# An attention, experts and feed-forward kernel on one core: six tiles for the factors made in the experts, a store on another queue, and other begin times for conversions

## The chip, the cores and the metric

The kernel runs on one core of a Trainium2 chip. The core has five engines that work side by side, each through an instruction queue of its own: TensorE (PE in the profile, its weight loads apart as PEld), VectorE (DVE), ScalarE (ACT), GpSimd (POOL) and SyncE (SP), which only issues transfers. An instruction waits at the head of its queue until the semaphores that it names have come, and what stands behind it on the same engine waits too. The metric is device time in microseconds, the median of several runs. The chip grants TensorE a clock at one of two levels, 1.2 or 2.4 GHz; the profile writes them as 0.50 and 1.00 of full speed.

## The reference, cut to what matters

```python
# q, k, v: (4, 8, 576, 64)
scores = 1.0 / np.sqrt(64) * np.matmul(q, k.transpose(0, 1, 3, 2))
thresh = np.max(scores, axis=-1, keepdims=True) - tau
scores = np.where(scores >= thresh, scores, -1000000000.0)
attn = softmax(scores)
x = np.matmul(attn, v) as (2304, 512)                  # tokens by model width

expert_idx = np.argmax(xn @ en.T / mtau, axis=1)       # one of 8 experts a token
for e in range(8):
    mask = expert_idx == e
    out[mask] = gate_w[mask, None] * (np.maximum(x[mask] @ w1[e], 0) @ w2[e])   # 512 -> 1024 -> 512

h = out @ w_in                                         # 512 -> 2048
g = np.maximum(h, 0.0) + alpha * np.minimum(h, 0.0)
return g @ w_out                                       # 2048 -> 512
```

w_in and w_out come as 64-bit floats; the kernel reads them as pairs of 32-bit words and turns them into float32 with integer operations ("conversion" below).

## The kernel before

**Products in two parts.** A float32 operand is kept as two tiles of a reduced type (fp32r): a high part, which ScalarE writes by a cast, and a low part, which GpSimd or VectorE writes as the difference of the value and its high part. A product takes three matmuls: high x high, high x low, low x high.

**Three stages.** Attention runs to about 354 us of the span, the experts from there to 641, the feed-forward network ("the network") to 1053; the rest is the end of the last stores.

**Experts.** There are 8 experts of fixed capacity (432, 256, 384, 256, 368, 272, 320 and 288 columns, in the order in which they run), each with 8 feature blocks: 64 groups g = 8 r + f. In group g, `l1(g)` multiplies by a block of w1, `relu` makes the high part `h` on ACT (L1209) and the low part on VectorE (L1210), and `l2(g-1)` multiplies the `h` of the group before by a block of w2 (L1257 to L1259). `wsplit` makes the high and low parts of the weights (L1124, L1138, L1139). After the last block the result is copied to `yT` (L1268, L1269) and `yout` (L1279) stores it in DRAM at a place that is read from `meta_i` first (L1278); both go through SP's queue. For the last expert that happens after the loop.

Preparations for the network are strewn between the groups. `conv` (conversion of w_in, L1605 to L1646) is called at fixed groups. Everything that stands in the list `early` has a due time in groups, given by `at(due, step)`, and is emitted in the loop as soon as g has reached it. In this list are the **factors**: the network multiplies by sums and differences of quarters of w_in, seven a pair of feature blocks, each 128 x 512 with both parts. For four of the eight pairs they are made here. `sums` forms them; `factor(i, p)` then has three steps: a cast of the high part on ACT (L1696), the subtraction on GpSimd (L1698), the store to the DRAM tensor `ws` by SP (L1700). Each takes a tile of `wtile`, here from a pool `wf` of two:

```python
for x, p in enumerate((1, 2, 4, 6, 7, 5, 3)):
    f = run(lambda i=i, p=p: factor(i, p))
    for y in range(3):
        at(g0 + 2.2 + 1.1 * x + 0.5 * y, f)
```

Later entries of `early` fetch the network's first inputs and call `weights` (L1711) five times, which loads a factor back from `ws` into the pool `wr` of `NR` = 6 tiles.

**Network.** It goes in six visits, `VISITS = ((0,0), (1,0), (2,0), (2,1), (1,1), (0,1))`: (block q of 768 tokens, half of the feature pairs), four pairs a visit. A pair takes seven products (`prod`, L1869, in the order p = 1, 2, 6, 7, 5, 3, 4, six matmuls of 384 columns each) which run up in two PSUM banks `ha` and `hb`; after each, the load of the factor that is needed five products later is issued (`weights`). ACT keeps partial results by copies `v`, `w`, `d` (L1878). `act` applies the activation with its alpha (`u` and `c`, L1891 to L1902), then ACT casts the high part `gh` (L1913) and GpSimd makes the low part `gl` (L1918). The output products (`f2mm`, L1985 to L1987, nine matmuls for one feature block and half a token block) of the pair or of the one before stand between the seven products. After the last feature block `evac` scales by the gate weight and `put` (L1950) or a plain store writes the rows.

Side work is held in chains of steps. `tick(us)` is called after each product (1.05) and after each set of output products (2.08 each feature block) and emits the next step or steps of each chain, as far as a small account of each engine's time allows; a step of kind "N" does nothing and ends the chain's turn for this tick. `finish(name)` emits at once whatever is left of a chain, where its result is needed. Two kinds of chains matter here. `wout(c)` converts one row block of w_out: a load (L2003), then nine steps on ACT, VectorE and GpSimd (L1605 to L1618), of which L1612 on ACT writes the high part and L1617 and L1618 on GpSimd the low part of `wo`. No more than two of them are open at a time. `factors(i)` makes the factors of one of the other four pairs: step k of nine casts factor k on ACT (L2041), subtracts for factor k - 1 on GpSimd (L2045) and stores factor k - 2 (L2047); its tiles come from a pool `wf` of three. The table `work` says in which visit, and at which pair, a chain is queued.

## Time and profile before

| | |
|---|---|
| timed runs, us | 1060.70, 1063.87, 1064.52 (median 1063.87) |
| the profiled execution: time / span, us | 1062.55 / 1060.6 |
| TensorE busy | 977.0 us, 92% of the span |
| VectorE busy | 785.4 us, 74% |
| ScalarE busy | 619.9 us, 58% |
| GpSimd busy | 682.7 us, 64% |
| mean granted clock of TensorE | 0.97 |

The span runs from the first instruction to the last of the one execution that the profiler recorded; the time of the same execution is 1.95 us longer. Busy times leave out waiting, so the shares say only which engine has least to spare over the whole. Where an engine stood still, and for whom, is read from the views by stretch, from the list of waits and from the timeline. There an idle time stands in brackets behind the instruction that ended it, with an arrow to what released it. Several matmuls of one line are drawn together as "x6"; ends of matmuls are modelled.

### The profile page before, as it was taken

To read this page: it belongs to the slowest core of one execution; us is meant where nothing else is said; L and a number is where in the kernel's file an instruction comes from. 1 tells how busy PE (TensorE), PEld (TensorE's weight loads), DVE (VectorE), ACT (ScalarE), POOL (GpSimd) and SP (SyncE) were. 2 spreads that over 40 slices of the span, in tenths; PEclk is the share of its full clock that TensorE was granted. 3 is DMA by queue.
4 is the path that set the end of the run, shared out by engine and by line. 5 is a ranking of instruction groups with operands and counts; after the bars stand their busy time and mean duration, and the time that the engine had idled before them with its cause. 6 is when DMAs were issued, how large, how long until landed. Compare 5 with 4: busy or idle time off the path is not lost. (4 is left out here: it accounts for less than half of the span.)

```text
span 1060.6 us, 18417 instructions
## 1 busy us (share of the span) xinstructions
PE 977.0 (92%) x6099; PEld 900.1 (85%) x6099; DVE 785.4 (74%) x1431; ACT 619.9 (58%) x1419; POOL 682.7 (64%) x654
## 2 busy tenths in 40 slices
PE   7999999899997897898897998979999998899994
PEld 6999999899996797898787997868888997788883
DVE  7999999999998585778486875685683676738533
ACT  6899998899986444544545555556674533424220
POOL 6988898989997143545497544573865556736523
PEclk9999999999998899899998999989999998999998
DMA  3333547434541857678676665646775676464641
GB/s 83 100 90 89 162 129 214 126 100 141 140 125 69 302 187 238 226 250 259 216 233 237 224 177 172 215 123 198 239 230 176 219 236 201 135 229 143 187 133 63
DMA packets 119161, 186.06 MB, mean 175 GB/s; under 512 B 24024, under 2 KB 50936, under 8 KB 119056
## 3 DMA queue, kind: packets, MB, share of 16 engines
q1 hardware_dynamic: 115456, 175.07, 53.3%
q0 software_dynamic: 3456, 9.59, 2.4%
q8 instruction: 51, 0.84, 0.3%
q14 instruction: 54, 0.44, 0.1%
q10 hardware_dynamic: 144, 0.13, 0.0%
HBM read 127.48 MB, written 48.41 MB: 166 GB/s over the span
## 5 line engine op out<-in xcount | busy, mean ns | idle before, releaser
L1918 POOL TENSOR_TENSOR gl<-c,gh 128x384 fp32r<-128x384 f32 x96 | 111.3, 1161 | 158.2 <-ACT gh L1913 140.9
L446 POOL TENSOR_TENSOR ptl<-x,pth 128x512 fp32r<-128x512 f32 x97 | 124.7, 1286 | 6.8
L1869 PE MATMUL ha<-x,wr 128*128 128x384 f32 x576 | 118.7, 341 | 8.7 <-ACT w L1878 5.1
L1226 PE MATMUL l<-x,w 128*128 128x256 f32 (+6 forms) x744 | 123.1, 316 | 0.0
L650 DVE SCALAR_TENSOR_TENSOR p<-s,mx,e 128x576 f32<-128x576 f32 x144 | 116.5, 812 | 7.1 <-ACT e L643 3.1
L1987 PE MATMUL o<-wo,gl 128*128 128x512 f32 x288 | 115.8, 402 | 4.8 <-POOL gl L1918 4.8
L1869 PEld LDWEIGHTS ha<-x,wr 128*128 128x128 f32 x576 | 104.5, 190 | 18.3 <-ACT w L1878 5.5
L1986 PE MATMUL o<-wo,gh 128*128 128x512 f32 x288 | 115.5, 401 | 4.6 <-POOL wo L1618 4.6
L1985 PE MATMUL o<-wo,gh 128*128 128x512 f32 x288 | 115.0, 399 | 3.8 <-ACT wo L1612 3.0
L1226 PEld LDWEIGHTS l<-x,w 128*128 128x128 f32 x744 | 115.6, 196 | 0.6
L634 DVE TENSOR_REDUCE mx<-s 128x1 f32<-128x576 f32 x144 | 108.5, 753 | 7.8 <-PE s L627 4.9
L663 PE MATMUL t<-ident,p 128*128 128x128 f32 (+1 forms) x720 | 111.8, 276 | 2.3 <-ACT x L689 0.9
L643 ACT ACTIVATE e<-s,mx 128x576 f32<-128x576 f32 x144 | 106.3, 739 | 6.5 <-DVE mx L634 6.0
L1257 PE MATMUL y<-h,w 128*128 128x256 f32 (+6 forms) x256 | 84.5, 330 | 21.4 <-ACT h L1209 21.4
L1258 PE MATMUL y<-h,w 128*128 128x256 f32 (+6 forms) x256 | 83.5, 326 | 5.8 <-DVE h L1210 4.9
L1869 PE MATMUL hb<-x,wr 128*128 128x384 f32 x432 | 86.9, 335 | 2.0 <-DMA wr<-ws 1.5
L1913 ACT CAST gh<-c 128x384 fp32r<-128x384 f32 x96 | 49.1, 515 | 66.7 <-DVE c L1902 50.5
L663 PEld LDWEIGHTS t<-ident,p 128*128 128x128 f32 (+1 forms) x720 | 80.7, 137 | 8.3 <-ACT x L689 2.2
L627 PE MATMUL s<-ks,qs 128*128 128x288 f32 x256 | 82.7, 338 | 3.0 <-ACT qs L534 1.4
L1259 PE MATMUL y<-h,w 128*128 128x256 f32 (+6 forms) x256 | 81.6, 319 | 0.0
L1869 PEld LDWEIGHTS hb<-x,wr 128*128 128x128 f32 x432 | 75.9, 188 | 3.1 <-issue 1.8
L707 PE MATMUL v<-pth,hlv 128*128 128x288 f32 (+2 forms) x256 | 75.2, 316 | 2.2 <-DVE run L953 1.0
(274 smaller groups left out, 2599.8 us busy)
## 6 DMA issues: line engine op xcount, KB each, us to landing
wr<-ws SPq DMA_DIRECT2D x168, 256.0 KB, 3.0
stg<-in_moe_w_dram SPq DMA_DIRECT2D x34, 512.0 KB, 4.3
stg<-in_moe_w_dram SPq DMA_DIRECT2D x15, 1024.0 KB, 6.1
ws<-wf SPq DMA_DIRECT2D x56, 256.0 KB, 3.7
kx<-ks SPq DMA_DIRECT2D x60, 144.0 KB, 2.6
xd<-zt SPq DMA_DIRECT2D x33, 256.0 KB, 2.8
raw<-yt_d SPq DMA_DIRECT2D x10, 768.0 KB, 7.2
cr<-in_moe_w_out_dram SPq DMA_DIRECT2D x12, 512.0 KB, 5.7
```

The lines of the kernel that those rows point to most:

```text
L446: lambda: nc.gpsimd.tensor_tensor(lo, raw, hi.bitcast(F32), op=ALU.subtract))
L634: nc.vector.tensor_reduce(out=mx[:, 0:1], in_=st["s", t][:, :, 0:288], op=ALU.min, axis=AX.XY)
L643: nc.scalar.activation(e, st["s", t][:, :, 0:288], AF.Exp, bias=st["mx", t][:, 0:1], scale=-1.0)
L650: nc.vector.scalar_tensor_tensor(out=p.rearrange("q (a b) -> q a b", a=2), in0=st["s", t][:, :, 0:288], scalar=st["mx", t][:, 2:3], in1=st ...
L663: nc.tensor.transpose(m[0:w, j * n + i * 128:j * n + (i + 1) * 128], st["p", t][:, c * 128:c * 128 + w], ident)
L1226: nc.tensor.matmul(m[:, 0:n], w[:, a, c], st["x"][:, b, c, 0:n], start=(i == 0), stop=(i + 1 == len(terms)))
L1257: nc.tensor.matmul(m[:, 0:n], w[:, 0, dsl], h[:, 0, 0:n], start=(f == 0), stop=False)
L1869: nc.tensor.matmul(m, w[:, a, k], x[:, b, k], start=start and n == 0, stop=n + 1 == len(terms), skip_group_check=not start)
L1918: P.tensor_tensor(gl, c, gh.bitcast(F32), op=ALU.subtract)
L1985: nc.tensor.matmul(m, gh[:, ts], WO[f][:, 0, :], start=first and x == 0, stop=False)
L1986: nc.tensor.matmul(m, gh[:, ts], WO[f][:, 1, :], start=False, stop=False)
L1987: nc.tensor.matmul(m, gl[:, ts], WO[f][:, 0, :], start=False, stop=n[0] == full and x + 1 == len(gs))
```

## The change

Five edits:

1. In the experts a factor's tile comes from the pool `wr` (six tiles, idle until the network's first loads) and no longer from the pool `wf` of two, which is gone there. The three steps of one factor are due 1 group apart, not 0.5; consecutive factors stay 1.1 groups apart.
2. `yout` of the last expert reads its place and stores through ACT's queue, not SP's.
3. In visit 0 the four conversions of w_out are all queued at the first pair, not one a pair.
4. In the chain of `factors` an empty step follows only every second of the nine, where it followed each.
5. At the very end, of the two sets of output products for the second half of the tokens, that of block `f1` goes first.

```diff
--- before.py
+++ after.py
@@ -1065,7 +1065,6 @@
         sm_p = mpool("sm", bufs=1)
         if not general:
             y2["wa"] = mpool("wa", bufs=1)
-            y2["wf"] = mpool("wf", bufs=2)
         stg_p = mpool("stg", bufs=2)
 
         def small(shape, dt=F32):
@@ -1275,8 +1274,9 @@
             if not general:
                 if i == 0:
                     n = CAPS[r]
-                    base = nc.sync.value_load(meta_i[0:1, MB + r:MB + r + 1], min_val=0, max_val=NT)
-                    nc.sync.dma_start(yt_d[:, :, bass.ds(base, n), :], st["yT"][:, :, 0:n, :])
+                    eng = nc.scalar if r + 1 == NE else nc.sync
+                    base = eng.value_load(meta_i[0:1, MB + r:MB + r + 1], min_val=0, max_val=NT)
+                    eng.dma_start(yt_d[:, :, bass.ds(base, n), :], st["yT"][:, :, 0:n, :])
                 return
             t0, tn = ntile(r)[i]
             m = ps_x.tile([128, 512], F32, tag="x", name="x")
@@ -1690,7 +1690,7 @@
 
         def factor(i, p):
 
-            t, flat, home = wtile(y2["wf"], "wf", i, p)
+            t, flat, home = wtile(wr_p, "wr", i, p)
             src = SUM[i][p]
             hi, lo = (t[:, x].rearrange("p (k j) -> p k j", k=2) for x in range(2))
             nc.scalar.copy(hi, src)
@@ -1767,7 +1767,7 @@
             for x, p in enumerate((1, 2, 4, 6, 7, 5, 3)):
                 f = run(lambda i=i, p=p: factor(i, p))
                 for y in range(3):
-                    at(g0 + 2.2 + 1.1 * x + 0.5 * y, f)
+                    at(g0 + 2.2 + 1.1 * x + y, f)
         y2["na"] = na = xa_p.tile([128, KF2], F32, name="na")
         nc.vector.tensor_scalar(out=na, in0=alpha_t, scalar1=-1.0, scalar2=None, op0=ALU.mult)
         at(53.1, lambda: fetch(0, 0))
@@ -2051,7 +2051,7 @@
             steps = [("W", 0, lambda: not made), ("S", 0, load)] + [("N", 0, nothing)] * 3
             steps += [("V", 0.8, lambda k=k: nth(k)) for k in range(4)] + [("N", 0, nothing)]
             for k in range(9):
-                steps += [("P", 0.95, lambda k=k: next_(k)), ("N", 0, nothing)]
+                steps += [("P", 0.95, lambda k=k: next_(k))] + [("N", 0, nothing)] * (k % 2)
             chain(4, steps, ("f", i))
 
         def xsplit(p, e):
@@ -2093,7 +2093,7 @@
         def xdiff_after_six():
             chain(2, [("N", 0, nothing)] * 2 + [("P", 2.15, lambda: (finish(("x", 6)), diff(4, P)))], ("d", 4))
 
-        work = {0: [("o", NV + x, x) for x in range(NQH)], 1: [("f", NQH, 0), ("f", NQH + 1, 2)] + [("o", 8 + x, x) for x in range(3)],
+        work = {0: [("o", NV + x, 0) for x in range(NQH)], 1: [("f", NQH, 0), ("f", NQH + 1, 2)] + [("o", 8 + x, x) for x in range(3)],
                 2: [("f", NQH + 2, 0), ("f", NQH + 3, 2), ("o", 11, 0), ("o", 12, 3)], 3: [("o", 13, 0), ("o", 14, 1), ("o", 15, 2)]}
 
         xsplit(3, "V")
@@ -2149,8 +2149,8 @@
                 step(4)
                 if (v, i) != (NVIS - 1, NQH - 1):
                     f2mm(v, (f0,), 0)
+        f2mm(v, (f1,), 1)
         f2mm(v, (f0,), 1)
-        f2mm(v, (f1,), 1)
         f2mm(v, (f0, f1), 0)
         f2.close()
 
```

Lines of the changed kernel after 1068 are lower by one, up to `yout`. TensorE's instructions keep their order, apart from edit 5.

SP's queue at the start of the network, before. `gs` is a small table of tokens and gates, `meta_i` the table of places, `yt_d` the experts' result in DRAM, `cr` the raw words of w_out:

```order
L1786 DMA gs<-pd 128x18x2
L1278 TENSOR_LOAD meta_i
L1278 ISA x2
L1279 ISA
L1279 DMA yt_d<-yT 256x1x576
L1711 DMA wr<-ws 128x512
L2003 DMA cr<-in_moe_w_out_dram 128x1024
L1711 DMA wr<-ws 128x512 x7
```

The same stretch of SP's queue now:

```order
L1786 DMA gs<-pd 128x18x2
L1711 DMA wr<-ws 128x512
L2003 DMA cr<-in_moe_w_out_dram 128x1024 x2
L1711 DMA wr<-ws 128x512 x10
L2003 DMA cr<-in_moe_w_out_dram 128x1024
L1711 DMA wr<-ws 128x512 x3
```

The place's load and the store have gone from it, and a second load of w_out stands in front of the factor loads. The pair is found in ACT's queue, behind two of the copies into `yT` and ahead of the first copy of the network:

```order
L1268 COPY yT<-y_8869 128x288
L1268 COPY yT<-y_8877 128x288
L1278 TENSOR_LOAD meta_i
L1278 ISA x2
L1279 ISA
L1279 DMA yt_d<-yT 256x1x576
L1878 COPY v<-ha 128x384
```

ACT now issues the store between the experts' last copies and the copy `v` of the first product.

GpSimd's queue at the start of visit 1, before. `t2` and `x5` belong to the next block of tokens, `f` and `wo7` to the conversion of row block 7 of w_out (numbers at names count tiles):

```order
L1734 TENSOR_TENSOR t2_9603<-raw_9487,t2_9603 128x768
L1743 TENSOR_TENSOR x5_9744<-t1_9574,x5_9744 128x768
L1918 TENSOR_TENSOR gl_9787<-c_9739,gh_9786 128x384
L1918 TENSOR_TENSOR gl_9801<-c_9768,gh_9800 128x384
L1617 TENSOR_TENSOR f_9725<-f_9725,wo7_9727 128x512
L1618 TENSOR_TENSOR wo7_9727<-f_9725,r_9726 128x512
L1918 TENSOR_TENSOR gl_9853<-c_9783,gh_9852 128x384
L1918 TENSOR_TENSOR gl_9880<-c_9834,gh_9879 128x384
```

The same stretch now:

```order
L1617 TENSOR_TENSOR f_9540<-f_9540,wo7_9542 128x512
L1734 TENSOR_TENSOR t2_9642<-raw_9495,t2_9642 128x768
L1743 TENSOR_TENSOR x5_9746<-t1_9596,x5_9746 128x768
L1918 TENSOR_TENSOR gl_9788<-c_9742,gh_9787 128x384
L1918 TENSOR_TENSOR gl_9802<-c_9768,gh_9801 128x384
L1618 TENSOR_TENSOR wo7_9542<-f_9540,r_9541 128x512
L1918 TENSOR_TENSOR gl_9839<-c_9784,gh_9838 128x384
```

L1617 of `wo7` moved up in front of `t2`, two `gl` and `x5`; L1618 stays behind the two `gl` it stood behind.

ACT's queue in the middle of visit 3, where the casts of the last `factors` chain stand, before:

```order
L1913 CAST gh<-c 128x384 x2
L1878 COPY v<-ha 128x384
L1913 CAST gh<-c 128x384
L2041 CAST wf<-wa 128x256 x2
L2041 CAST wf<-sum 128x256 x4
L2041 CAST wf<-wa 128x256
L1878 COPY w<-ha 128x384
L1913 CAST gh<-c 128x384
```

The casts of the last such chain now, in visit 2, with other work between:

```order
L2041 CAST wf<-wa 128x256 x2
L1878 COPY d<-ha 128x384
L2041 CAST wf<-sum 128x256 x2
L1895 ACTIVATE u<-c 128x384
L1896 ACTIVATE c<-c 128x384
L1612 CAST wo_11105<-f 128x512
L1895 ACTIVATE u<-ha 128x384
L1896 ACTIVATE c<-ha 128x384
L2041 CAST wf<-sum 128x256 x2
L1913 CAST gh<-c 128x384 x2
L1895 ACTIVATE u<-c 128x384
L2041 CAST wf<-wa 128x256
```

The row of seven casts has become four groups of two, two, two and one with copies and activations between them.

## Rows read from the trace of the kernel before

**Rows 1.** Windows view: us, busy us (instructions) by engine, PEclk, DMA share, GB/s

```profile
354.00:641.00 287.00, 258.18 (x1629) 246.37 (x1630) 206.51 (x328) 139.54 (x308) 150.55 (x123) 0.96 0.70 229
641.00:1053.00 412.00, 386.67 (x1873) 341.35 (x1871) 256.94 (x337) 178.75 (x359) 226.91 (x186) 0.98 0.58 186
```

**Rows 2.** The list of waits: who waited <- for whom: us, times, longest

```profile
ACT wf L1696 <- DMA ws<-wf: 60.7, 15, 9.3
...
PE y L1257 <- ACT h L1209: 21.4, 9, 4.1
```

**Rows 3.** Timeline of ACT, then PE: start, us, instruction [idle before <- releaser]

```profile
424.21 0.40 ACT L1696 CAST wf<-sum 128x256 fp32r<-128x256 f32 x1 [7.79 <-DMA ws<-wf]
...
424.95 0.38 PE L1257 MATMUL y<-h,w 128*128 128x256 f32 x1 [3.79 <-ACT h L1209]
```

**Rows 4.** Windows view of six stretches of 3.4 us, the first and the sum

```profile
426.40:429.80 3.40, 3.40 (x17) 3.23 (x16) 0.20 (x1) 0.54 (x2) 1.95 (x2) 0.50 0.49 168
...
sum 20.40, PE 20.21 PEld 19.86 DVE 14.42 ACT 10.80 POOL 15.24; mean PE 3.37 PEld 3.31 DVE 2.40 ACT 1.80 POOL 2.54
```

**Rows 5.** The view of line L1696: xcount: ns min/median/max, first to last start

```profile
L1696 ACT CAST wf<-sum x16: 404/406/440, 411.6 to 579.4; 128x256 fp32r<-128x256 f32 x16
L1696 ACT CAST wf<-wa x12: 404/408/426, 395.6 to 553.1; 128x256 fp32r<-128x256 f32 x12
```

**Rows 6.** Windows view of the fourth and the sixth expert

```profile
469.30:501.90 32.60, 28.05 (x206) 26.59 (x205) 28.59 (x51) 16.11 (x36) 19.40 (x20) 0.95 0.81 252
543.80:583.30 39.50, 31.27 (x206) 29.22 (x205) 25.53 (x40) 18.99 (x44) 30.07 (x27) 0.91 0.71 240
```

**Rows 7.** Timeline of DVE in the fourth expert, the same subtraction twice

```profile
469.10 1.74 DVE L1139 TENSOR_TENSOR w<-stg,w 128x512 fp32r<-128x512 f32 x1
...
476.94 0.69 DVE L1139 TENSOR_TENSOR w<-stg,w 128x512 fp32r<-128x512 f32 x1
```

**Rows 8.** Waits and timeline of SP's queue, then timeline of PE, network's start

```profile
SPq L1279 <- DVE yT L1269: 12.1, 1, 12.1
...
641.65 0.63 SPq L1279 DMA_DIRECT2D yt_d<-yT  x1
...
647.83 1.28 PE L1869 MATMUL ha<-x,wr 128*128 128x384 f32 x6 [1.57 <-DMA wr<-ws]
...
650.64 1.28 PE L1869 MATMUL hb<-x,wr 128*128 128x384 f32 x6 [1.53 <-DMA wr<-ws]
```

**Rows 9.** Timeline of PE at the start of visit 1

```profile
703.06 1.33 PE L1869 MATMUL hb<-x,wr 128*128 128x384 f32 x6
...
707.34 0.79 PE L1985 MATMUL o<-wo,gh 128*128 128x512 f32 x1 [2.95 <-ACT wo L1612]
...
711.81 0.80 PE L1986 MATMUL o<-wo,gh 128*128 128x512 f32 x1 [3.67 <-POOL wo L1618]
...
715.39 1.73 PE L1869 MATMUL ha<-x,wr 128*128 128x384 f32 x6
```

**Rows 10.** Timeline of PE in visit 3

```profile
875.04 1.20 PE L1869 MATMUL hb<-x,wr 128*128 128x384 f32 x6
...
883.41 2.29 PE L1869 MATMUL ha<-x,wr 128*128 128x384 f32 x6 [5.08 <-ACT w L1878]
...
888.35 1.23 PE L1869 MATMUL ha<-x,wr 128*128 128x384 f32 x6
...
900.91 1.21 PE L1869 MATMUL ha<-x,wr 128*128 128x384 f32 x6
...
904.05 1.21 PE L1869 MATMUL ha<-x,wr 128*128 128x384 f32 x6
```

**Rows 11.** The view of line L2047, its last line

```profile
DMA to landing us min/median/max: 2.0/3.1/5.2
```

**Rows 12.** Timeline of PE at the end of the network

```profile
1037.26 0.50 PE L1985 MATMUL o<-wo,gh 128*128 128x512 f32 x1 [0.87 <-ACT gh L1913]
...
1038.49 0.50 PE L1987 MATMUL o<-wo,gl 128*128 128x512 f32 x1 [0.50 <-POOL gl L1918]
```

## The prediction

> **What bounds the kernel now.** I read first the busy time by stretch, then who waited for whom, then TensorE's clock, then the timeline around each longer wait. The change leaves attention alone, so two stretches matter. In the experts (354 to 641 us) TensorE is busy 258.18 of 287.00 us, in the network (641 to 1053 us) 386.67 of 412.00 [rows 1]: in both no other engine is nearer to full, and what can be won is TensorE's idle time and the time at which its clock is down. The list of waits says who causes it. In the experts ScalarE (ACT) stands still 60.7 us, in 15 pieces, for the store of a factor tile to land, and TensorE stands still 21.4 us, in 9 pieces, for ACT's relu `h` [rows 2]. One piece in the timeline ties the two: ACT waits 7.79 us in front of a factor's cast, and TensorE 3.79 us for the `h` queued behind that cast [rows 3]. The relu comes after the cast in ACT's queue; two tiles are too few for stores that take microseconds to land.
>
> Behind each of six such stops lies a stretch of 3.4 us in which the granted clock is 0.50, the lower of the two levels (1.2 of 2.4 GHz); together TensorE is busy 20.21 us there [rows 4]. At full clock that work takes half, so 10.1 us are lost on top of the idle time.
>
> **The change part by part.** All sums are made against the profiled execution, 1062.55 us (its span is 1060.6); the median of the three timed runs, 1063.87, is 1.3 above it, which is inside their spread.
>
> *Factors in the experts in six tiles; cast, subtraction and store a group apart.* The 28 casts, 28 subtractions and 28 stores stay, with the same shapes. What goes is ACT's wait: the tile that a cast needs was stored two casts ago, and now six casts ago. The 28 casts start between 395.6 and 579.4 us [rows 5], 6.8 us apart on average; four casts more are some 27 us, and even at half that spacing the longest wait seen, 9.3 us [rows 2], is covered. Without the wait `h` follows its product, so the 21.4 us and the 10.1 us at the lower clock go: 31.5. What is late next? VectorE and GpSimd. In the fourth expert (469.3 to 501.9 us) VectorE is busy 28.59 of 32.60 us, in the sixth (543.8 to 583.3) GpSimd 30.07 of 39.50 [rows 6]; the same subtraction on VectorE took 0.69 us alone and 1.74 beside GpSimd [rows 7]. A shorter stretch packs these two closer. I leave 1 us for waits that form again and take **30.5**; bounds 15 (rival 1) and 36 (TensorE's smaller waits for VectorE shrink too). The later store also stands later in SyncE's (SP's) queue, in front of weight loads; it now waits less for its subtraction, so I count nothing for that.
>
> *The last expert's result on ACT's queue.* SP stood 12.1 us in front of this store, for VectorE's copy into `yT`; the store went out at 641.65, taking 0.63 us, ahead of the next factor load. TensorE then waited 1.57 and 1.53 us for factor loads [rows 8]. Moved, SP issues that load as soon as the experts allow it. But two loads of w_out now stand between the first and the second factor load, where there was one, and the DMA engines get the same bytes in a shorter time. Gain between 1 and 3.1; I take **2.5**. ACT pays a register load and 0.63 us of issue, and queued behind it is the copy `v` of the first product, which the third product needs. ACT waits for the same copy as SP did and is free some 0.7 us after 641.6, while the third product begins two products of about 1.05 us after the first: cost 0, at most 1.
> The Trainium skill (DMA: Bandwidth & Descriptors, Issuing engines are not separate DMA queues) says that issuing from several engines saves only the sequencer's issue time, usually small beside the transfer. By that rule this edit would give 0.6 us. The trace differs in what the queue held up, 12.1 us of waiting against 0.63 of issue, so I keep the 2.5.
>
> *All four conversions of w_out begun in the first pair of visit 0.* They were begun one a pair, and the last (`wo7`) was needed at the start of visit 1, where its two last steps were still to do. There TensorE waited 2.95 us for ACT's half and 3.67 for GpSimd's, at the lower clock. From the second product (703.06) to the third (715.39) went 12.33 us, with nine output products between. The ordinary distance over such nine is 904.05 - 900.91 = 3.14 [rows 9, 10]. So 9.2 us are lost. After the change only GpSimd's last step of `wo7` is left at that place, behind two `gl`; VectorE has five steps less in that stretch, so those come earlier. I expect 0 to 2 us to remain and take **8**, bounds 5 and 9.7. The work itself moves into pairs 0 to 2 of visit 0; ACT, VectorE and GpSimd have room there, but a `gl` may come late behind a conversion: cost **1**, bounds 0 and 4.
>
> *Factors in the network: two steps in a tick instead of one in two ticks.* Before, the last of the four was unfinished when visit 3 needed it, and its seven casts went out in one row, each behind its store, with TensorE's product waiting 5.08 us behind them. From the fourth product (875.04) to the fifth (883.41) went 8.37 instead of 3.14, from there to the sixth (888.35) 4.94 instead of 3.14 [rows 10]: 7.0 lost. Now every chain ends well before it is needed, so **7** is won. The price: there are still three tiles here, and the order puts the casts in pairs, the second of each pair needing the store that stands just in front of it. Such a store takes 3.1 us to land, 5.2 at most [rows 11]. It is issued when a subtraction of the tick before ends, so ACT, which has two activations and a copy to do meanwhile, waits some 1 to 2 us, twice a chain. Behind it in ACT's queue stand `gh` and the copy `v`, which have 2 to 3 us before TensorE asks for them. Four chains: cost **2**, bounds 0 and 10.
>
> *The last output products swapped.* At the end TensorE waited 0.87 us for `gh` and 0.50 for `gl` of the feature block that is finished last [rows 12]. The other block is ready earlier and now goes first: **1.4**, bounds 1 and 1.4. What follows keeps its order.
>
> **Sum.** 30.5 + 2.5 + 8 + 7 + 1.4 - 1 - 2 = 46.4, and 1062.55 - 46.4 = 1016.2. I say **1016**. With every term at its better end 57.2, thus 1005; with the dearer ends of the network's terms and the experts' 25 some 36, thus 1026.
>
> **The rivals.**
> 1. *VectorE and GpSimd take the place of ACT's wait in the experts.* For: the busy shares of rows 6 and the slower subtraction of rows 7. Against: in the stretches with the long waits VectorE itself was idle behind ACT. If half of the term is given back, it is 15 instead of 30.5, and the time 1031.5.
> The Trainium skill (SBUF — State Buffer, A bandwidth-pool intuition that's wrong) says that GpSimd and a two-port operation of VectorE do not share but block each other. By that rule this rival is the likelier the closer the stretches are packed. The trace has 25.53 and 30.07 us busy within 39.50, so at least 16.1 us lie side by side, some of it blocked time; it bears the rule out in part, and I raised this rival's chance for it.
> 2. *The paired casts reach TensorE once in each chain*, at the price of the row of casts seen before, 7.0: 28 us instead of 2, thus 1042. Against: that row held seven casts without anything between; now two stand together.
> 3. *Six tiles do not do what they say*, because the store, a group later and behind SP's loads, lands too late all the same. If a third of ACT's waits stays, 10 us come back: 1026.
> 4. *Slower than before.* All twelve casts that follow their store closely (three in each of four chains) stop TensorE. At 5.2 us for the landing and 1.7 for the clock each costs 6.9, together 83, thus about 1097. It decides from 48.4 / 12 = 4.0 us a cast on. Against: before, the same casts with the same three tiles showed hardly any wait outside the one row.
>
> **Chances.** Forecast 0.70, rival 1 0.15, rival 2 0.07, rival 3 0.05, rival 4 0.03. The range that should hold 8 in 10 goes from 1005 less a us to rival 1 with dearer costs in the network: 1004 to 1034. A measurement tells about 0.5% (5 us) from no change. All cases but the last are faster by more; a little of it may end near nothing: faster 0.96, same 0.02, slower 0.02.
>
> **What would show it.** Right: in the experts ACT's wait for stores of factors under 5 us, TensorE's idle time for `h` under 6, and at most two stretches at the lower clock instead of six; the last load before the first product no longer waited for; no idle TensorE over 2 us at the start of visit 1 nor in the middle of visit 3; the end shorter by 1.4. Wrong: an unchanged idle time of TensorE in the experts, now put down to VectorE's half of `h` or to GpSimd's half of a weight (rival 1), or ACT's waits in front of the network's casts growing from a few us to tens, with TensorE idle behind `v`, `w` or `gl` (rivals 2 and 4).

## The result

| | before | changed |
|---|---|---|
| median of the timed runs, us | 1064.19 (1060.70 to 1065.78) | 1019.32 (1016.71 to 1021.69) |
| ratio, 95% interval | 1 | 0.9582 (0.9545 to 0.9619) |
| profiled execution: time / span, us | 1062.55 / 1060.6 | 1021.06 / 1019.2 |
| TensorE busy | 977.0 us, 92% | 961.3 us, 94% |
| mean granted clock | 0.97 | 0.981 |

The forecast was 1016 with a range of 1004 to 1034. The time lies 3 us above the forecast, but the parts of the sum did not all come out as put: two were off by 2 to 4 us in the profiled execution, and there the fourth edit gained nothing. The profiled execution is 1.7 us longer than the median.

The experts and the network again as two stretches (us; busy us and instructions of PE, PEld, DVE, ACT, POOL; granted clock; share of the DMA engines; GB/s), the network now beginning at 610:

```profile
354.00:610.00 256.00, 245.01 (x1640) 236.44 (x1639) 220.46 (x329) 140.26 (x310) 152.87 (x123) 1.00 0.82 260
610.00:1011.00 401.00, 385.50 (x1873) 340.69 (x1871) 255.82 (x337) 177.49 (x359) 226.17 (x185) 0.99 0.58 188
```

Against [rows 1] the experts are 31 us shorter, the network 11. In the experts TensorE stands still for 11 us, where it was 29, and the clock is up throughout. From the list of waits of the changed kernel (who waited <- for whom: us, times, longest), where lines of the experts are lower by one than before:

```profile
ACT h L1208 <- PE l L1225: 90.7, 53, 3.6
...
PE y L1257 <- DVE h L1209: 6.7, 8, 1.5
...
ACT wf L2041 <- DMA ws<-wf: 5.4, 3, 2.2
```

The 60.7 us in which ACT waited for stores in the experts, and TensorE's 21.4 us for `h` [rows 2], are not in it any more. ACT's cast of `h` waits more for TensorE, 90.7 us where it was 67.5. Most of what is left in the experts is TensorE's wait for VectorE's low half of `h`, 6.7 us. The last two of these waits were there before, too:

```profile
PE y L1258 <- DVE h L1210: 4.9, 8, 1.4
...
ACT wf L2041 <- DMA ws<-wf: 4.3, 5, 1.6
```

Each has grown a little.

TensorE executes the same products in both kernels, so the start of one matmul in each trace tells where time was gained: of a product its first one, of the last set of output products its last one. The table takes the difference between marks, all from the two profiled executions:

| mark (a product on TensorE) | before, us | changed, us | gained since the mark above | forecast |
|---|---|---|---|---|
| twelfth matmul of the experts' first weight block | 361.67 | 361.38 | 0.3 | 0 |
| first product of the network | 640.85 | 609.89 | 30.7 | 30.5 |
| second pair of visit 0 | 653.85 | 620.27 | 2.6 | 2.5 |
| first product of visit 1 | 702.00 | 668.16 | 0.3 | -1 |
| third product of visit 1 | 715.39 | 675.67 | 5.9 | 8 |
| second pair of visit 2 | 791.33 | 758.05 | -6.4 | -2 |
| second pair of visit 4 | 927.40 | 887.98 | 6.1 | 7 |
| first product of the last pair | 1022.63 | 983.21 | 0.0 | 0 |
| last output product | 1051.21 | 1009.66 | 2.1 | 1.4 |
| sum | | | 41.6 | 46.4 |

The rest of the span, behind the last output product, is 9.4 us before and 9.5 now. Each column is one execution, and the stretches at the lower clock do not fall alike in every execution, so a row is good to 1 to 3 us; where single edits below give more executions of the same stretch, they are named.

**The network's start.** Timelines of TensorE, then of ACT's queue and ACT, in the changed kernel:

```profile
615.98 1.31 PE L1869 MATMUL ha<-x,wr 128*128 128x384 f32 x6 [0.57 <-ACT d L1878]
617.14 1.20 PE L1869 MATMUL hb<-x,wr 128*128 128x384 f32 x6
...
610.69 0.67 ACTq L1279 DMA_DIRECT2D yt_d<-yT  x1
611.46 0.48 ACT L1878 COPY v<-ha 128x384 f32<-128x384 f32 x1 [1.35 <-PE ha L1869]
```

The two waits for factor loads [rows 8] are gone, and the store costs ACT 0.67 us in a moment in which it would have waited for TensorE anyway: `v` comes as soon as its product is there.

**The start of visit 1.** TensorE, then GpSimd:

```profile
669.23 1.20 PE L1869 MATMUL hb<-x,wr 128*128 128x384 f32 x6
...
672.89 0.50 PE L1986 MATMUL o<-wo,gh 128*128 128x512 f32 x1 [2.22 <-POOL wo L1618]
...
675.67 1.95 PE L1869 MATMUL ha<-x,wr 128*128 128x384 f32 x6
...
668.36 2.93 POOL L1918 TENSOR_TENSOR gl<-c,gh 128x384 fp32r<-128x384 f32 x2 [1.04 <-ACT gh L1913]
671.25 1.58 POOL L1618 TENSOR_TENSOR wo<-f,r 128x512 fp32r<-128x512 f32 x1
```

ACT's half is in time now, GpSimd's is not: the step of `wo7` starts at 671.25, behind the two `gl`, for which GpSimd itself had waited 1.04 us. From the second to the third product it takes 6.44 us instead of 12.33 [rows 9]; the ordinary distance is 3.14 [rows 10].

**Visits 1 and 2, where time was lost.** ACT and TensorE at the start of visit 2:

```profile
750.21 0.40 ACT L2041 CAST wf<-sum 128x256 fp32r<-128x256 f32 x1 [2.23 <-DMA ws<-wf]
750.52 1.26 ACT L1939 ACTIVATE os<-o,gs 128x512 f32<-128x512 f32 x2
751.67 0.48 ACT L1878 COPY d<-ha 128x384 f32<-128x384 f32 x1
...
752.20 2.17 PE L1869 MATMUL ha<-x,wr 128*128 128x384 f32 x6 [1.76 <-ACT d L1878]
```

A cast of the second chain of factors waits 2.23 us for the store of its tile. Behind it ACT scales two outputs, and only then copies `d`, for which TensorE waits 1.76 us; 3.4 us at the lower clock follow. A pair earlier, in the last of visit 1, TensorE waits for `d` too, behind casts that split the next tokens:

```profile
733.05 0.89 ACT L1741 CAST x<-raw 128x768 fp32r<-128x768 f32 x1
733.84 0.46 ACT L1878 COPY d<-ha 128x384 f32<-128x384 f32 x1
...
734.36 1.33 PE L1869 MATMUL ha<-x,wr 128*128 128x384 f32 x6 [1.54 <-ACT d L1878]
```

How much is lost here depends on the clock. Four of the single edits below leave the second chain where it is (the store back on SP, the conversions one a pair, the last sets swapped back, the last `gl` ahead of the stores). In their traces the stretch of the table's row takes 79.2 to 80.2 us, so 3.3 to 4.2 more than before and not 6.4. TensorE stands still as long in them (3.9 to 4.7 us, 4.5 in the changed kernel, 0.9 before). But there it is at the lower clock for at most 0.8 us, and in the changed kernel for 5.0, of which 1.6 still belong to the wait at the start of visit 1.

### The profile page after: what moved, and what is told of

Its sections match the earlier page's. It is cut to its first block, busy times and chain, and to the rows that moved or that the text cites. A ratio compares the mean times of both kernels' runs of the same rounds, so it can differ in the third digit from the quotient of the medians.

```text
span 1019.2 us, 18395 instructions
## 1 busy us (share of the span) xinstructions
PE 961.3 (94%) x6099; PEld 887.6 (87%) x6099; DVE 797.7 (78%) x1431; ACT 618.6 (61%) x1419; POOL 684.9 (67%) x654
## 5 line engine op out<-in xcount | busy, mean ns | idle before, releaser
L1918 POOL TENSOR_TENSOR gl<-c,gh 128x384 fp32r<-128x384 f32 x96 | 109.1, 1140 | 139.9 <-ACT gh L1913 122.1
L1225 PE MATMUL l<-x,w 128*128 128x256 f32 (+6 forms) x744 | 118.7, 308 | 0.0
L1225 PEld LDWEIGHTS l<-x,w 128*128 128x128 f32 x744 | 110.7, 188 | 0.6
L1257 PE MATMUL y<-h,w 128*128 128x256 f32 (+6 forms) x256 | 80.4, 314 | 6.9 <-DVE h L1209 6.7
L1208 ACT ACTIVATE h<-l 128x256 fp32r<-128x256 f32 (+6 forms) x64 | 28.3, 442 | 92.3 <-PE l L1225 90.7
L1256 PE MATMUL y<-h,w 128*128 128x256 f32 (+6 forms) x256 | 82.3, 321 | 2.0 <-ACT yT L1268 1.6
L1258 PE MATMUL y<-h,w 128*128 128x256 f32 (+6 forms) x256 | 79.1, 309 | 0.0
```

What stands on the lines that cost most here:

```text
L1225: nc.tensor.matmul(m[:, 0:n], w[:, a, c], st["x"][:, b, c, 0:n], start=(i == 0), stop=(i + 1 == len(terms)))
L1918: P.tensor_tensor(gl, c, gh.bitcast(F32), op=ALU.subtract)
```

## The experiments

Times of single kernels are compared with the kernel before in the same session (medians 1063.52, 1065.22, 1062.79 and 1062.39 us); for differences of a few us the marks of the table above are used. Kernels for which a ratio is given were timed four or five times, the others once. The four times of the changed kernel lie between 1016.7 and 1021.7 us, so single times that differ by less than 5 us say nothing by themselves.

### Is it the tiles? Four kernels on the first edit

**Six tiles, wider spacing, nothing else.**

```diff
-            y2["wf"] = mpool("wf", bufs=2)
...
-            t, flat, home = wtile(y2["wf"], "wf", i, p)
+            t, flat, home = wtile(wr_p, "wr", i, p)
...
-                    at(g0 + 2.2 + 1.1 * x + 0.5 * y, f)
+                    at(g0 + 2.2 + 1.1 * x + y, f)
```

> The kernel before with the first edit alone: six tiles and the steps of a factor a group apart. My theory, that ACT's wait for the stores of two tiles is what holds TensorE up in the experts: ACT's waits for stores of factors, 60.7 us in 15 pieces before, go to under 5; the last expert ends some 31 us earlier, as in the changed kernel; the network keeps its 412 us; time near 1032. Rival, that VectorE and GpSimd take the place of that wait: the last expert ends 15 us earlier, time near 1048. Second rival, that the experts' gain depends on the other edits: less than 25 us earlier.

Measured: 1032.43 us, ratio 0.9717 (0.9694 to 0.9741). The list of waits has no ACT wait for stores of factors in the experts. From the first mark of the table to the network's first product it takes 248.4 us, where the kernel before takes 279.2 and the changed one 248.5; from there to the last output product 409.5, against 410.4 before. The experts of this kernel:

```profile
354.00:610.00 256.00, 244.99 (x1642) 236.66 (x1641) 220.81 (x330) 140.85 (x310) 152.74 (x123) 1.00 0.78 258
```

So the whole gain of the experts comes from this edit, and VectorE and GpSimd do not give it back.

**Six tiles, the old spacing.**

```diff
-            y2["wf"] = mpool("wf", bufs=2)
...
-            t, flat, home = wtile(y2["wf"], "wf", i, p)
+            t, flat, home = wtile(wr_p, "wr", i, p)
```

> The kernel before with the six tiles alone, the three steps of a factor still half a group apart. If the tiles do it: ACT's wait for stores gone, the last expert ends 31 us earlier within 3, time near 1032. If the wider spacing does it (a cast, a subtraction and a store that follow one another too closely hold up ACT, GpSimd and SP's queue whatever the number of tiles): less than half of that, time 1045 or more, with waits of GpSimd for the cast and of SP for the subtraction that hold up other work.

Measured: 1029.26 us. The experts take 246.3 us from the first mark up to the network's first product. The wider spacing is not needed; it is no better than the old one.

**Two tiles, the wider spacing.**

```diff
-                    at(g0 + 2.2 + 1.1 * x + 0.5 * y, f)
+                    at(g0 + 2.2 + 1.1 * x + y, f)
```

> The kernel before with the wider spacing alone, still two tiles. From the cast that uses a tile again back to its store there are then 0.2 groups where there were 1.2. If the tiles do it: every cast meets a store that has only just been issued, 26 casts wait for a landing of 4.6 us (median of these stores before) less about 1 us, some 90 us of waits in place of 60.7, and the time goes up, 1070 to 1095. If the spacing does it: time near 1035.

Measured: 1127.22 us, much slower than even the tiles theory had it. Its list of waits and its windows:

```profile
ACT wf L1696 <- DMA ws<-wf: 129.6, 19, 11.0
...
PE y L1257 <- ACT h L1209: 56.7, 14, 6.6
...
PE y L1257 <- ACT yT L1269: 10.2, 2, 5.9
```

```profile
354.00:705.00 351.00, 276.76 (x1643) 263.60 (x1643) 199.13 (x329) 140.29 (x310) 146.45 (x123) 0.87 0.59 188
```

The direction is that of the tiles theory, the size is not. ACT waits 129.6 us where some 90 were expected, and I had not counted what that does to TensorE and its clock. TensorE waits 56.7 us for `h` instead of 21.4, and 10.2 us for copies into `yT`. The stretch is 64 us longer than before [rows 1]. TensorE is busy 18.6 us longer in it with the same matmuls (276.76 against 258.18), and stands still 45.4 us longer. The longer busy time is the clock. The stretches at the lower level in the experts, fourteen of them, have this sum:

```profile
sum 88.40, PE 59.97 PEld 57.66 DVE 43.77 ACT 36.60 POOL 27.79; mean PE 4.28 PEld 4.12 DVE 3.13 ACT 2.61 POOL 1.98
```

Half of the 59.97 us in which TensorE is busy there is lost, 30.0 us, where it was 10.1 before [rows 4].

**Four tiles.** The lines of the first of these kernels, and of the six places every third stays empty:

```diff
+            y2["made"] = y2.get("made", 0) + 1
+            if y2["made"] % 2 == 0:
+                wtile(wr_p, "wr", i, p)
```

> The kernel before with the wider spacing and four tiles in turn (the pool of six, with one place left empty after every second factor). From a cast back to the store of its tile there are 2.4 groups, some 10 us, against the longest landing of 7.4 us. If what counts is this distance: ACT's wait for stores under 10 us, and 25 to 31 us gained, time 1031 to 1037. If SP's queue delays the stores by more than a group: waits of 20 us or more stay.

Measured: 1031.26 us; no wait of ACT for these stores is left, and the experts take 248.4 us, as with six. The distance from a store to the next cast into its tile orders all of these kernels. With n tiles it is 1.1 n groups less the store's own delay: 0.2 groups in the kernel with two tiles and wide steps (129.6 us of waits), 1.2 before (60.7), 2.4 with four (none), 4.6 and 5.6 with six (none). A group is 287/64 = 4.5 us long before, and 248.4/64 = 3.9 us with four tiles. From issue to landing these stores took before:

```profile
DMA to landing us min/median/max: 3.4/4.6/7.4
```

1.2 groups (5.4 us) cover the median and not the longest; 2.4 (9.3 us) cover the longest too. The kernel with four tiles shows no landing times of its own; with six tiles at the old spacing the longest was 8.3 us.

### The last expert's store back on SP

```diff
-                    eng = nc.scalar if r + 1 == NE else nc.sync
+                    eng = nc.sync
```

> The changed kernel with the last expert's store back on SP's queue. My theory, that the store held up the factor loads behind it for as long as it waited itself: TensorE waits 1 to 3 us for factor loads at the network's first products, and from the second product of the network on everything is 2 to 3 us later than in the changed kernel. Rival, that only the 0.6 us of issue time count: at most 0.6 us later there.

Measured: 1022.89 us. SP and TensorE in this kernel:

```profile
610.18 0.63 SPq L1279 DMA_DIRECT2D yt_d<-yT  x1
610.86 0.59 SPq L1711 DMA_DIRECT2D wr<-ws  x1
611.55 1.41 SPq L2003 DMA_DIRECT2D cr<-in_moe_w_out_dram  x2
...
615.98 1.31 PE L1869 MATMUL ha<-x,wr 128*128 128x384 f32 x6 [1.19 <-DMA wr<-ws]
...
619.47 2.26 PE L1869 MATMUL hb<-x,wr 128*128 128x384 f32 x6 [2.19 <-DMA wr<-ws]
```

From the network's first product to its second pair it takes 14.79 us, where the changed kernel takes 10.38 and the kernel before 13.00. So the edit is worth 4.4 us between these two executions. In 2.8 of them TensorE stands still, and 1.6 are the lower clock, which here follows the second wait (0.50 for 3.4 us from 619.3). Where the conversions are queued one a pair, and so one load of w_out less stands there, the edit is worth 1.7 to 2.1: 12.09, 12.13 and 12.47 us in the kernels with six or four tiles and the store on SP, against 10.42 in the next experiment, store on ACT. The kernel with two tiles and wide steps, which has one load less as well, takes 14.63, and there too the clock fell. So it is not shown that the second load makes the store dearer: TensorE stands still for 3.4 us with it, for 2.2 to 3.1 without. In the changed kernel SP issues both loads before the network begins:

```profile
606.91 0.81 SPq L2003 DMA_DIRECT2D cr<-in_moe_w_out_dram  x2
```

The Trainium skill (DMA: Bandwidth & Descriptors, Issuing engines are not separate DMA queues) says that a second issuing engine saves only issue time. Here the issue takes 0.63 us and the edit gives 1.7 at the least: what counts is not the time of issue but that the store waits at the head of a queue for its data, 12.7 us in this kernel, with the loads behind it.

### Conversions of w_out one a pair again

```diff
-        work = {0: [("o", NV + x, 0) for x in range(NQH)], ...
+        work = {0: [("o", NV + x, x) for x in range(NQH)], ...
```

> The changed kernel with the four conversions of w_out queued one a pair again. My theory: the two waits at the start of visit 1 (for ACT's and for GpSimd's half of the last conversion) come back, 6.6 us where 2.2 are left in the changed kernel, with some 10 us at the lower clock; the third product of visit 1 stands 6 us later against the first of visit 0 than in the changed kernel. Rival, that the earlier conversions cost visit 0 something: the stretch of visit 0 is shorter by 1 us or more here.

Measured: 1024.02 us. TensorE at the start of visit 1:

```profile
673.79 0.50 PE L1985 MATMUL o<-wo,gh 128*128 128x512 f32 x1 [2.97 <-ACT wo L1612]
...
678.26 0.79 PE L1986 MATMUL o<-wo,gh 128*128 128x512 f32 x1 [3.97 <-POOL wo L1618]
```

From the second to the third product of visit 1 it takes 12.24 us, as before (12.33), against 6.44 in the changed kernel. Visit 0 is not shorter: from its second pair to visit 1 it takes 48.18 us here and 47.89 in the changed kernel. The earlier conversions cost nothing there.

### The factors' steps slow again

```diff
-                steps += [("P", 0.95, lambda k=k: next_(k))] + [("N", 0, nothing)] * (k % 2)
+                steps += [("P", 0.95, lambda k=k: next_(k))] + [("N", 0, nothing)]
```

> The changed kernel with an empty step after each step of the factors again. The changed kernel loses 6 to 7 us against the kernel before from the second pair of visit 1 to the middle of visit 2 (waits for copy d of ACT of 1.54 and 1.76 us, and 3.4 us at the lower clock). Theory, that this is the price of the faster chains: the loss is gone here, and the wait in visit 3, some 7 us with the lower clock, is back, so the time stays within 2 us. Rival, that the loss comes from the conversions being earlier: it stays here, and the time is 7 us longer.

Measured: 1020.03 us (span 1018.2), as the changed kernel. From the third product of visit 1 to the second pair of visit 2 it takes 75.71 us, where the changed kernel takes 82.38 and the kernel before 75.94: the loss is gone. In visit 3 the wait is back:

```profile
843.26 2.05 PE L1869 MATMUL ha<-x,wr 128*128 128x384 f32 x6 [4.79 <-ACT w L1878]
```

So the fourth edit removed one stop and made others. In the profiled execution of the changed kernel they are of the same size; in the four traces with 79.2 to 80.2 us they are 1 to 3 us smaller than what was won in visit 3.

### The chains elsewhere, the steps still fast

```diff
-        ... 1: [("f", NQH, 0), ("f", NQH + 1, 2)] + [("o", 8 + x, x) for x in range(3)],
-        2: [("f", NQH + 2, 0), ("f", NQH + 3, 2), ("o", 11, 0), ("o", 12, 3)], 3: [("o", 13, 0), ...
+        ... 1: [("f", NQH, 0)] + [("o", 8 + x, x) for x in range(3)],
+        2: [("f", NQH + 1, 0), ("f", NQH + 2, 2), ("o", 11, 0), ("o", 12, 3)], 3: [("f", NQH + 3, 0), ("o", 13, 0), ...
```

> The changed kernel with the second chain of factors queued at the first pair of visit 2 instead of the third of visit 1, the third at the third pair of visit 2, the fourth at the first of visit 3. If the loss in visits 1 and 2 comes from where the second chain lies (its sums on VectorE beside the splits of the next tokens in the last pair of visit 1, its waiting casts in front of ACT's scaling of outputs at the start of visit 2): 5 to 6 us gained, time 1013 to 1015. If it comes from the paired casts as such: the stops move along with the chains, and the time stays within 2 us of the changed kernel; a fourth chain that ends too late would show as a wait of 5 us or more in visit 3.

Measured: 1014.13 us. The loss is gone (75.01 us over the same stretch), and visit 3 has no such wait. ACT still waits for stores of the network's factors, but not where TensorE needs it:

```profile
ACT wf L2041 <- DMA ws<-wf: 3.6, 3, 1.9
```

Three casts wait, as in the changed kernel, and TensorE's longest wait from the third product of visit 1 to the last pair is 1.3 us. The third and the fourth chain moved by two pairs as well. It is the place of the second chain that cost 6.4 us there (3.3 to 4.2 in the four other traces), not the pairing of casts: its sums on VectorE lay beside the splits of the next tokens in the last pair of visit 1, its waiting cast in front of the scaling of the outputs of the visit before. Which share each of the two has was not separated.

### The last sets of output products swapped back

```diff
-        f2mm(v, (f1,), 1)
         f2mm(v, (f0,), 1)
+        f2mm(v, (f1,), 1)
```

> The changed kernel with the two last sets of output products in the old order. My theory, that the block finished last then meets its gh and gl too early: waits of 0.9 and 0.5 us come back in front of that set, and the last output product is 1 to 1.5 us later against the product before those sets. Rival: the wait of 3.1 us for the last gl, which stands behind three stores on GpSimd, takes it up, and nothing changes at the last output product.

Measured: 1019.89 us, too close to tell by itself. From the first product of the last pair to the last output product it takes 29.44 us, in the changed kernel 26.45, before 28.58. The waits are back as forecast:

```profile
993.62 0.51 PE L1985 MATMUL o<-wo,gh 128*128 128x512 f32 x1 [0.87 <-ACT gh L1913]
...
994.86 0.50 PE L1987 MATMUL o<-wo,gl 128*128 128x512 f32 x1 [0.51 <-POOL gl L1918]
```

The clock makes the difference larger than the waits. It falls behind the later wait of 3.13 us for the last `gl`, and stays down for 6.8 us here and for 3.4 in the changed kernel. Five traces with the old order, the kernel before and the four of the first edit, take 28.5 to 28.6 us for this stretch; the changed kernel and four others with the new order take 26.4 to 26.6. So the edit is worth 2.0 to 2.2.

### The last gl ahead of the stores

```diff
         f2mm(v, (f1,), 1)
+        for x in ((f0, 1), (f0, 0), (f1, 0)):
+            finish(("g", v) + x)
         f2mm(v, (f0,), 1)
```

> The changed kernel with the activations of the last feature blocks finished before the output products whose results are stored: on GpSimd the last gl then stands ahead of the three stores. In the changed kernel this gl starts at 1004.38, while its gh was ready at 1000.05, and TensorE waits 3.14 us for it, with 3.4 us at the lower clock behind. If the queue behind the stores is what costs it: the wait falls under 0.5 us, the last output product is 4 to 5 us earlier against the ones before, and the time 3 to 5 us shorter. Rival, that the stores decide the end: they start later, and the time stays within 1 us.

Before and after the change the longest wait near the end is the same, 3.1 us. In the changed kernel (TensorE, then GpSimd):

```profile
1005.46 0.79 PE L1987 MATMUL o<-wo,gl 128*128 128x512 f32 x1 [3.14 <-POOL gl L1918]
...
1003.40 0.98 POOL L1950 DMA_INDIRECT out_dram<-os,gs  x1 [0.30 <-issue]
1004.38 1.02 POOL L1918 TENSOR_TENSOR gl<-c,gh 128x384 fp32r<-128x384 f32 x1
```

Measured: 1014.84 us. GpSimd now:

```profile
998.36 1.02 POOL L1918 TENSOR_TENSOR gl<-c,gh 128x384 fp32r<-128x384 f32 x1 [1.09 <-ACT gh L1913]
999.53 0.99 POOL L1950 DMA_INDIRECT out_dram<-os,gs  x1
```

The stretch from the first product of the last pair to the last output product is 21.75 us instead of 26.45, and the span is 1013.0 instead of 1019.2. 4.7 us of that come from this edit; most of the rest is that in this execution no stretch at the lower clock followed the wait at the start of visit 2. The six stores stand close together at the end, but they hold up little: behind the last output product the span takes 9.8 us, and 9.5 in the changed kernel.

### All together, twice

The moved chains, the last `gl` ahead of the stores, and the eighth conversion ahead of other side work:

```diff
-            chain(3, [("W", 0, lambda: len(open_) < 2), ...
+            chain(1 if c == 2 * NV - 1 else 3, [("W", 0, lambda: len(open_) < 2), ...
```

> The changed kernel with the chains of factors moved as in the run before with moved chains, the last gl ahead of the stores, and the conversion of the eighth row block of w_out put ahead of other side work. Expected: 7 us from the chains, 4 from the end, and 2 to 4 at the start of visit 1, where TensorE waits 2.2 us for this conversion and then has 3.4 us at the lower clock; time 1004 to 1008, ratio to the kernel before 0.944 to 0.949. If one wait only takes the place of another at the start of visit 1 (two gl now stand behind a conversion's last step): 1007 to 1010.

Measured: 1009.71 us, ratio 0.9506 (0.9487 to 0.9525). That is the second of the two expectations. The chains and the end bring what they brought alone; the conversion does not. The eighth is done earlier, but the seventh is now last, and TensorE waits for that one, a set of output products sooner:

```profile
668.30 0.50 PE L1986 MATMUL o<-wo,gh 128*128 128x512 f32 x1 [2.40 <-POOL wo L1618]
```

GpSimd was the full engine there, busy 18.47 of 20 us around that place in the changed kernel (the last of the five busy times):

```profile
655.00:675.00 20.00, 17.78 (x85) 15.48 (x84) 16.82 (x16) 13.57 (x25) 18.47 (x11) 0.97 0.53 170
```

Here another order of its work only changed which result was late. So the last kernel takes work from it, with the conversions in their old order:

```diff
-                    if p == 5:
-                        xsplit(5, "P")
+                        xsplit(5, "P" if v else "V")
```

> The changed kernel with the chains of factors moved and the last gl ahead of the stores, as in the run with all of these together, but with the conversions of w_out in their old order, and with the low part of one of the next tokens' inputs (x5) made by VectorE instead of GpSimd in visit 0; on GpSimd the last step of the eighth conversion then stands ahead of the two gl. If GpSimd's load in the last pair of visit 0 is what makes this conversion late: the wait of 2.2 us at the start of visit 1 falls under 0.5 us and the lower clock behind it goes, 3 to 4 us, time 1005 to 1007, ratio to the kernel before 0.945 to 0.949. Rival, that VectorE is as full there: a wait for c or gl of 1.5 us or more takes its place, and the time is 1008 to 1011.

Measured: 1004.71 us, ratio 0.9464 (0.9441 to 0.9488), the best of the study. GpSimd and then TensorE at the same place:

```profile
663.34 2.02 POOL L1618 TENSOR_TENSOR wo<-f,r 128x512 fp32r<-128x512 f32 x1
667.33 2.93 POOL L1918 TENSOR_TENSOR gl<-c,gh 128x384 fp32r<-128x384 f32 x2 [1.97 <-ACT gh L1913]
...
667.86 1.20 PE L1869 MATMUL hb<-x,wr 128*128 128x384 f32 x6
...
669.13 0.40 PE L1986 MATMUL o<-wo,gh 128*128 128x512 f32 x1
...
670.98 1.23 PE L1869 MATMUL ha<-x,wr 128*128 128x384 f32 x6
```

The conversion's last step ends 4 us before TensorE asks for it, and from the second to the third product it takes 3.12 us, the ordinary distance. VectorE made the low part in 2.05 us and nothing waits for it. On GpSimd the step now also stands ahead of the two `gl`, so the load taken off and the new order were not separated. In the network TensorE is now busy 378.93 of 385 us at full clock:

```profile
609.00:994.00 385.00, 378.93 (x1871) 336.85 (x1869) 255.24 (x338) 177.73 (x358) 224.39 (x183) 1.00 0.59 195
```

## Why the prediction was right, and where not

- **The six tiles (30.5; measured 30.7).** Right, and for the reason given: the edit alone does it, four tiles do as well, and two with the wider spacing go the other way. That the size fits so well is in part luck. I took 20.4 us of idle time and 10.1 of clock; measured, TensorE stands still 18.2 us less and is busy 12.4 us less. Its wait for VectorE's `h` has grown by 1.8 us, from 4.9 to 6.7, where I left 1 and gave 6 as the sign, and 1.6 us for a copy into `yT` are new. Two readings were not exact, without weight in the sum: of the six stretches at the lower clock [rows 4] the one at 433.2 stands behind a wait of 1.40 us for VectorE's `h`, not for ACT's; and the subtraction of 0.69 us [rows 7] was not alone, as GpSimd worked beside it for 0.5 us. Rivals 1 and 3 are out.
- **The store on ACT (2.5; measured 2.6).** Right in size and in mechanism: the two waits for factor loads went, and with the store back on SP they are there again. But 0.5 to 0.9 of the 2.6 came without this edit (13.00 before, 12.09 to 12.47 with six or four tiles and the store on SP). With the store back on SP the stretch is 1.8 us longer than before; 1.5 of these are longer busy time of TensorE, behind the fall of the clock in that execution, which the term left out. The second load of w_out in SP's queue, which I took as a small debit, was none: without the store ahead of it SP issued it before the network began.
- **The conversions (8 less 1; measured 5.9 plus 0.3).** The removed wait is right, the rest was at the bad end: I expected 0 to 2 us to remain for GpSimd's last step, and 2.22 us of waiting and the lower clock behind it left 3.3 us more than the ordinary distance. The sign of no idle time over 2 us is missed by this. I had counted VectorE's steps that come earlier, and not that GpSimd itself is the full engine in that stretch; what stood ahead of the step in the order was not only two `gl`, and a wait for their `gh`, but the splits ahead of those. The price in visit 0 that I put at 1 is nil.
- **The factors in the network (7 less 2; measured 6.1 less 6.4).** The stop in visit 3 was right. The price was not (6.4 in the profiled execution, 3.3 to 4.2 in the four other traces): rival 2 came true once. The step that failed is the sentence on what stands behind a waiting cast: I named `gh` and `v` with 2 to 3 us to spare, took it for every pair alike, and did not look at what else ACT and VectorE do where the second chain would come to lie. There ACT scales outputs and splits tokens, and there is nothing to spare. The bounds of 0 and 10 held it.
- **The swap (1.4; measured 2.1).** The waits are those that were read, 1.4 us of idle time. The other 0.7 is time in which TensorE is busy longer: a wait costs more than its idle time (by the trace the matmul before it runs out alone for 0.17 us, and the one that ends it is followed after 0.33 us instead of 0.23), and the stretch at the lower clock, which stands behind the wait of 3.1 us for the last `gl` in both kernels, holds 0.5 us less work. The term took a wait for its idle time alone.
- **Rival 4** priced such stops at 6.9 us each; the one that came cost about 2.6 us (from the start of visit 2 to its second pair), since only 3.4 us at the lower clock followed a wait of 1.8; in the four other traces, where no lower clock followed it, 0.7 to 0.9.
- The sum came out 5 us too high, and the median 3 us above the forecast. Two misses (conversions 2.1 less at the start of visit 1, factors 5.3 less) were partly paid back by the price in visit 0 and the swap. The lower end of 36 was added up wrongly: it takes the gains at their lower ends, but the two costs at 1 and 2. With their dearer ends, 4 and 10, it is 25, thus 1038, so the range was narrower than its own bounds.

## What to carry to other kernels

Count the tiles of a ring by the distance in time from a store's issue to the next write into its tile, and compare that with the longest landing, not the median: at 1.2 groups late stores stopped TensorE, which had nothing to do with them, nine times, at 2.4 never. A step that waits costs what stands behind it in its engine's queue at that place, so a chain of side work is judged where it comes to lie, not by how its steps follow one another: the same chain, queued two pairs later and begun 21 us later against visit 2, was free. Where an engine is nearly full over a stretch, a new order of its work may only change which result is late, as it did here; with one operation moved to another engine the wait went.

## What was not expected of the hardware

Short waits of TensorE cost more than their idle time, by its clock (lower level 1.2 of 2.4 GHz), but not every one does. In the kernel with two tiles and wide steps, 45.4 us more of standing still came with 18.6 us more of busy time over the same matmuls. Which wait is followed by a fall can't be told from its length in these traces. In the changed kernel a wait of 2.22 us at 672.89 was followed by 3.4 us of granted clock 0.50; the same wait of 2.22 us at 672.72 in the kernel with the last sets swapped back was not. A wait of 1.54 us at 734.36 was not followed by any, though one of 1.76 at 752.20 was, and the same wait of 1.66 us in the kernel with the last `gl` moved was not. In the kernel before a wait of 2.77 us at 410.4 left the clock up, and one of 1.40 at 432.3 did not. Even the same instructions come out differently. In the experts of the changed kernel TensorE waits 1.51 us at 545.0; with the last sets swapped back, which leaves the experts as they are, it waits 1.53 us at 544.9. The 3.4 us behind these two waits (the granted clock is the third number from the end):

```profile
545.00:548.40 3.40, 3.40 (x27) 3.40 (x28) 3.37 (x7) 3.25 (x9) 2.75 (x3) 1.00 1.05 405
```

```profile
545.20:548.60 3.40, 3.40 (x17) 3.40 (x16) 3.37 (x8) 2.74 (x7) 2.74 (x3) 0.50 1.05 407
```

So a single execution tells the idle time of a stop well, and its price by the clock only with luck.
